# Backward pass of a windowed attention: set-up, first four quads and last weight gradients in another form

## The chip, the core and the metric

The kernel runs on one core of a Trainium2 chip. A core has five engines with their own instruction streams: TensorE (PE) multiplies and transposes into PSUM, VectorE (DVE) and ScalarE (ACT) copy results out of PSUM and compute element by element, GpSimd (POOL) and SyncE (SP) here mostly issue DMAs; ACT issues some too. All DMAs of a core share 16 DMA engines. The metric is the device time of one execution in microseconds, lower is better: the median of several runs.

## The reference

The input x is an image of 256 x 256 pixels with C = 384 channels in bf16. It is cut into 1024 windows of 8 x 8 pixels; each window attends to itself, with one head. The kernel returns the output and the three gradients for a given `grad_out`.

```python
qkv = xw @ wqkv                       # xw: 1024 windows x 64 x 384
q, k, v = qkv[..., :C], qkv[..., C:2*C], qkv[..., 2*C:]
p = softmax(einsum('bqc,bkc->bqk', q, k) * C ** -0.5)
o = einsum('bqk,bkc->bqc', p, v) @ wo
out, vjp = jax.vjp(forward, x, wqkv, wo)
return out, *vjp(grad_out)            # d x, d wqkv, d wo
```

## The kernel before

**Algebra.** The weights are folded once: A = Wq Wk^T times the scale, AT is its transpose, B = Wv Wo, BT its transpose (C x C each, `A_sb`, `AT_sb`, `B_sb`, `BT_sb`). Scores are then x A x^T, the output P x B, and every gradient needs only x, `grad_out` and these four. The folding needs transposes of the three parts of `w_sb` (`wT`) and, for the end, of `wo_sb` (`woT_sb`): 36 transposes of 128 x 128 on TensorE against the identity `ident`, each group of three copied out of a PSUM bank by VectorE, and then four products of nine matmuls (L93 to L102).

**Quads.** The work goes over 128 quads. A quad is four tiles of 128 pixels, two windows each. `load` fetches x into `xq` (four DMAs of 96 KB on SP's queue) and `grad_out` into `dq` (four on POOL's). `load_turn` turns both into `dT` and `xT` (channels on the partitions) by two DMA transposes on SP's queue; the test on `G_ON_PE`, which is 0, leaves all of it to DMA, and `grad_turn`, which would do it on TensorE, does nothing.

**Steps.** `step(c, b, a, ahead)` handles three quads at once in an order written out by hand, which holds on every engine (`manual_schedule`): the quad b gets its scores (`sd`, 24 small matmuls), the softmax and its gradient on VectorE and ScalarE (`soft`, six parts), and `uq` and `vq` (x B and x AT, 24 matmuls of 384 columns, copied out by ScalarE); the quad a, one ahead, gets `z` (`project` kind 0: BT on `dT`, nine matmuls of 512 columns) and `y` (kind 1: A on `xT`, 18 of half the rows); both land in `yz`, which SP's queue turns into `tok`; the quad c, one behind, gets `attend`, which makes the output and d x and stores them from POOL's queue, and leaves `Uq` and `Wq`. `turn` sends the probabilities and their gradient (`ps`) through another DMA transpose on SP's queue to `PS`. The order of b's part, with the places that matter here:

```python
B(scores); B(soft, 0)
B(uv, 0, 0); B(uv, 0, 1); B(soft, 1)
B(uv, 1, 0); B(uv, 1, 1); B(soft, 2); B(soft, 3)
B(uv, 2, 0); B(uv, 2, 1)
for t in range(QUAD): A(grad_turn, t)
B(uv, 3, 0); B(uv, 3, 1); B(soft, 4)
for mo in range(CK): A(project, 0, mo)
B(soft, 5); B(turn)
```

So step i has on SP's queue, in this order: `dT` and `xT` of quad i + 2, `PS` of quad i, the loads of quad i + 3, `tok` of quad i + 1. A DMA that has to wait holds up all behind it on its queue.

**Weight gradients.** `gf_group` sums x^T U and x^T W over three quads into `GF_acc` (f32), in six pieces of 12 matmuls; `filler` puts two pieces into each step from step 4 on. The last group has only two quads. After the loop `filler` runs what is left, and then the code from L380 on casts `GF_acc` to `GFb`, turns it into `GFT` on TensorE, multiplies with the weights (27 and 9 matmuls) and stores d wqkv in three row blocks and d wo in one.

All PSUM tiles come from `ring`, eight banks.

Of the kernel before, what the change touches and what calls it, by code (L numbers as in the profile page):

```python
# [8 lines left out]
ACT = mybir.ActivationFunctionType  # L9
ALU = mybir.AluOpType  # L10
AX = mybir.AxisListType
BF16 = mybir.dt.bfloat16
F32 = mybir.dt.float32
# [9 lines left out]
def kernel(  # L23
# [33 lines left out]
    ring = ctx.enter_context(tc.tile_pool(name="ring", bufs=8, space=bass.MemoryType.PSUM))  # L57

    ident = const.tile([P, P], BF16)
    make_identity(nc, ident[:])  # L60

    w_sb = const.tile([P, CK, J], BF16)
    nc.sync.dma_start(out=w_sb[:], in_=wqkv.rearrange("(m p) j -> p m j", p=P))
    wo_sb = grp.tile([P, CK, C], BF16, tag="Wq", name="wo_sb")
    nc.scalar.dma_start(out=wo_sb[:], in_=wo.rearrange("(m p) n -> p m n", p=P))

    wT = []
    for part in range(3):
        dst = grp.tile([P, CK, C], BF16, tag="Uq", name="wT")
        for k in range(CK):  # L70
            jm = part * CK + k
            pt = ring.tile([P, C], BF16, tag="r")
            for m in range(CK):
                nc.tensor.transpose(pt[:, m * P:(m + 1) * P], w_sb[:, m, jm * P:(jm + 1) * P], ident[:])
            nc.vector.tensor_copy(out=dst[:, k, :], in_=pt[:])
        wT.append(dst)
    woT_sb = const.tile([P, CK, C], BF16)
    for mo in range(CK):
        pt = ring.tile([P, C], BF16, tag="r")
        for m in range(CK):  # L80
            nc.tensor.transpose(pt[:, m * P:(m + 1) * P], wo_sb[:, m, mo * P:(mo + 1) * P], ident[:])
        nc.vector.tensor_copy(out=woT_sb[:, mo, :], in_=pt[:])

    A_sb = const.tile([P, CK, C], BF16)
    AT_sb = const.tile([P, CK, C], BF16)
    B_sb = const.tile([P, CK, C], BF16)
    BT_sb = const.tile([P, CK, C], BF16)
    for dst, left, right, sc in (
        (BT_sb, wo_sb, wT[2], None),
        (A_sb, wT[0], wT[1], scale),  # L90
        (B_sb, wT[2], wo_sb, None),
        (AT_sb, wT[1], wT[0], scale),
    ):  # L93
        for mr in range(CK):
            pc = ring.tile([P, C], F32, tag="r")
            for mc in range(CK):
                nc.tensor.matmul(pc[:], lhsT=left[:, mc, mr * P:(mr + 1) * P], rhs=right[:, mc, :],
                                 start=(mc == 0), stop=(mc == CK - 1))
            if sc is None:
                nc.vector.tensor_copy(out=dst[:, mr, :], in_=pc[:])  # L100
            else:
                nc.scalar.activation(out=dst[:, mr, :], in_=pc[:], func=ACT.Copy, scale=sc)  # L102

    GF_acc = const.tile([P, 2, CK, C], F32)
    nc.vector.memset(GF_acc[:], 0.0)

    def windows(ap, st, first, count=2):
        row, col = st["at"]
# [10 lines left out]
            nc.gpsimd.dma_start(out=dq[:, t, :], in_=windows(grad_out, st, 2 * t))  # L119

    def load_turn(st):
        xq, dq = st["xq"], st["dq"]
        st["xT"] = xT = qp.tile([P, QUAD, CK, P], BF16, tag="xT", name="xT", bufs=3)
        st["dT"] = dT = qp.tile([P, QUAD, CK, P], BF16, tag="dT", name="dT")
        for src, dst in ((dq, dT), (xq, xT)):
            k = G_ON_PE if src is dq else 0
            if k < QUAD:
                nc.sync.dma_start_transpose(out=dst[:, k:].rearrange("p t m k -> p (t m) k"),
                                            in_=src[:, k:].rearrange("p t c -> p (t c)"))

    def grad_turn(st, t):
        if t >= G_ON_PE:
            return
        pt = ring.tile([P, CK, P], BF16, tag="r")
        for m in range(CK):
            nc.tensor.transpose(pt[:, m, :], st["dq"][:, t, m * P:(m + 1) * P], ident[:])
        nc.vector.tensor_copy(out=st["dT"][:, t, :, :], in_=pt[:])

    ALL = False
    split = [ALL]  # L140
# [152 lines left out]

    fill = []

    def gf_group(sts):
        n = len(sts) * QUAD
        for f in range(2):
            for ma in range(CK):
                pw = ring.tile([P, C], F32, tag="r", name="pg")  # L300
                for i in range(n):
                    st, t = sts[i // QUAD], i % QUAD
                    product(pw[:], st["xq"][:, t, ma * P:(ma + 1) * P], st["UW"[f] + "q"][:, t, :], i == 0, i == n - 1)
                nc.vector.tensor_tensor(out=GF_acc[:, f, ma, :], in0=pw[:], in1=GF_acc[:, f, ma, :], op=ALU.add)  # L304
                yield

    def filler(n):
# [7 lines left out]
    def step(c, b, a, ahead):  # L315


        def on(st):
            return (lambda f, *r: f(st, *r)) if st is not None else (lambda f, *r: None)
        C_, B, A = on(c), on(b), on(a)  # L320
        B(scores)
        B(soft, 0)
        B(uv, 0, 0)
        B(uv, 0, 1)
        B(soft, 1)
        B(uv, 1, 0)
        B(uv, 1, 1)
        B(soft, 2)
        B(soft, 3)
        B(uv, 2, 0)  # L330
        B(uv, 2, 1)
        for t in range(QUAD):
            A(grad_turn, t)
        B(uv, 3, 0)
        B(uv, 3, 1)
        B(soft, 4)
        for mo in range(CK):
            A(project, 0, mo)
        B(soft, 5)
        B(turn)  # L340
        if ahead is not None:
            load(ahead)
        filler(1)
        C_(attend, (0, 1))
        split[0] = True
        for mo in range(CK):
            A(project, 1, mo)
        A(to_tokens)
        filler(1)
        split[0] = ALL  # L350
        C_(attend, (2, 3))

    G_ON_PE = 0
    EV = {"z": "AAA", "y": "AAA", "u": "AAAA", "v": "AAAA", "o": "AAAA", "U": "DDDD", "W": "DDDD", "d": "AAAA"}
    quads = [(row, col) for row in range(0, H, 2 * WIN * QUAD) for col in range(0, W, WIN)]
    sts = [{"at": q, "i": i} for i, q in enumerate(quads)]
    n = len(sts)
    AHEAD = 3
    with tc.manual_schedule(engines=MANUAL):
        for i in range(min(AHEAD, n)):  # L360
            load(sts[i])
            if i < AHEAD - 1:
                load_turn(sts[i])
        held = []
        get = lambda i: sts[i] if 0 <= i < n else None
        for i in range(-1, n + 1):
            if AHEAD - 1 <= i + AHEAD - 1 < n:
                load_turn(sts[i + AHEAD - 1])
            step(get(i - 1), get(i), get(i + 1), get(i + AHEAD) if i >= 0 else None)
            if i > 0:  # L370
                held.append(sts[i - 1])
                sts[i - 1] = None
            if held and (len(held) == GQ or i == n):
                fill.append(gf_group(held))
                held = []
        split[0] = False
        filler(1 << 30)

    GFb, GFT = [], []
    for f in range(2):  # L380
        GFb.append(grp.tile([P, CK, C], BF16, tag="Uq", name="GFb"))
        GFT.append(grp.tile([P, CK, C], BF16, tag="Wq", name="GFT"))
        nc.vector.tensor_copy(out=GFb[f][:], in_=GF_acc[:, f, :, :])
        for mb in range(CK):
            pt = ring.tile([P, C], BF16, tag="r")
            for ma in range(CK):
                nc.tensor.transpose(pt[:, ma * P:(ma + 1) * P], GFb[f][:, ma, mb * P:(mb + 1) * P], ident[:])
            nc.vector.tensor_copy(out=GFT[f][:, mb, :], in_=pt[:])
    dw_view = out_2.rearrange("(m p) j -> p m j", p=P)
    for ma in range(CK):  # L390
        dw_sb = grp.tile([P, J], BF16, tag="xq", name="dw_sb", bufs=2 * GQ + 4)
        for i, (lhs, rhs, r0) in enumerate(((GFT[0], w_sb, C), (GFb[0], w_sb, 0), (GFT[1], woT_sb, 0))):
            pe = ring.tile([P, C], F32, tag="r")
            for mb in range(CK):
                nc.tensor.matmul(pe[:], lhsT=lhs[:, mb, ma * P:(ma + 1) * P], rhs=rhs[:, mb, r0:r0 + C],
                                 start=(mb == 0), stop=(mb == CK - 1))
            if i < 2:
                nc.scalar.activation(out=dw_sb[:, i * C:(i + 1) * C], in_=pe[:], func=ACT.Copy, scale=scale)
            else:
                nc.vector.tensor_copy(out=dw_sb[:, i * C:(i + 1) * C], in_=pe[:])  # L400
        nc.sync.dma_start(out=dw_view[:, ma, :], in_=dw_sb[:])
    dwo_sb = qp.tile([P, QUAD, C], BF16, tag="dq", name="dwo_sb", bufs=6)
    for mc in range(CK):
        pe = ring.tile([P, C], F32, tag="r")
        for ma in range(CK):
            nc.tensor.matmul(pe[:], lhsT=w_sb[:, ma, 2 * C + mc * P:2 * C + (mc + 1) * P], rhs=GFb[1][:, ma, :],
                             start=(ma == 0), stop=(ma == CK - 1))
        nc.vector.tensor_copy(out=dwo_sb[:, mc, :], in_=pe[:])
    nc.sync.dma_start(out=out_3.rearrange("(m p) n -> p m n", p=P), in_=dwo_sb[:, 0:CK, :])


# [28 lines left out]
```

## Time and profile before

| What | us |
|---|---|
| median of 7 runs | 1996.82 (1994.23 to 2000.95) |
| time of the profiled execution | 1995.6 |
| its span, first to last instruction | 1993.5 |
| TensorE busy | 1961.8 |
| ScalarE busy | 1453.8 |
| VectorE busy | 1258.2 |
| first transpose of weights on TensorE | at 6.32 |
| first `y` projection | at 19.84 |
| sum of the last gradient group on VectorE begun | at 1980.95 |
| last store issued | at 1990.17 |

The page of the profile gives busy time of each engine, the span in 40 slices, the DMA queues, and the chain of work that ended last. TensorE's time is the sum of matmuls whose ends are modelled, so being busy does not mean being at its peak. A row of a timeline reads: start, duration, engine, line, operation, output <- input, count, and in brackets the idle time before it with what ended it; on SP's queue the duration is the time for which the issue held the queue. The windows give busy time by stretch, with the granted TensorE clock as a share of full speed.

### The profile page before, as it was taken

What the parts mean: (1) busy time and instruction counts of PE and PEld (TensorE: products, weight loads), DVE (VectorE), ACT (ScalarE), POOL (GpSimd) and SP (SyncE); (2) the same over time, 40 slices, a digit from 0 to 9 for tenths busy, and PEclk for the clock granted to TensorE, in tenths of its full rate; (3) what the DMA queues carried; (4) which work ended last, traced back from release to release, by engine and by line L of the source; (5) the groups of instructions that cost most, each with busy time, mean ns of one, the idle gap of its engine ahead of it and who ended that gap; (6) DMA issues with size and microseconds to landing.
All of it is one profiled execution on the core that took longest, in us unless ns stands there. A gap on an engine that the chain in (4) does not pass through costs nothing.

```text
span 1993.5 us, 52374 instructions
## 1 busy us (share of the span) xinstructions
PE 1961.8 (98%) x19418; PEld 1123.2 (56%) x19418; DVE 1258.2 (63%) x2851; ACT 1453.8 (73%) x3341; POOL 1122.6 (56%) x2054
## 2 busy tenths in 40 slices
PE   7999999999999999999999999999999999999998
PEld 4455555555555555555555555555555555555555
DVE  4666666566666666666666666666666666666665
ACT  5777777677777777777777777777777777777774
POOL 3655555555555555555655565555555555555643
PEclk9999999999999999999999999999999999999999
DMA  9999999999999999999999999999999999999993
GB/s 198 216 216 226 210 223 209 210 217 221 211 223 216 222 209 215 220 224 211 227 211 214 223 206 224 220 219 219 220 216 214 209 224 219 220 218 215 216 207 100
DMA packets 1042272, 425.62 MB, mean 214 GB/s; under 512 B 925792, under 2 KB 1016672, under 8 KB 1042016
## 3 DMA queue, kind: packets, MB, share of 16 engines
q1 hardware_dynamic: 943312, 270.60, 81.4%
q0 software_dynamic: 98304, 151.39, 31.1%
q8 instruction: 152, 2.49, 0.5%
q14 instruction: 104, 0.85, 0.1%
q10 hardware_dynamic: 400, 0.29, 0.0%
HBM read 101.84 MB, written 101.84 MB: 102 GB/s over the span
## 4 chain that ended last, share of the span: by engine, by line
PE 90%; DMA 7%; ACT 1%; DVE 1%; issue 0%; SPq 0%; POOL 0%; ACTq 0%; POOLq 0%
PE pj L147 33%; PE pj L145 12%; PE pg L147 12%; PE pg L145 11%; PE pd L258 6%; PE pu L253 5%; PE sd L147 5%; PE pw L253 4%; DMA dT<-dq 4%; DMA PS<-ps 1%; DMA dq<-in_grad_out_dram 1%; ACT uq L229 0%; DMA xT<-xq 0%; ACT vq L229 0%; PE pd L253 0%
## 5 line engine op out<-in xcount | busy, mean ns | idle before, releaser
L292 POOL DMA_DIRECT2D out_dram<-o x256 | 139.1, 543 | 691.9 <-ACT o L264 679.7
L304 DVE TENSOR_TENSOR GF_acc<-pg,GF_acc 128x384 f32<-128x384 f32 x258 | 143.9, 558 | 527.2 <-PE pg L145 372.2
L264 ACT CAST o<-po 128x384 bf16<-128x384 f32 x512 | 221.4, 487 | 248.1 <-issue 247.7
L147 PEld LDWEIGHTS <-xT 128*128 128x128 bf16 x3072 | 291.7, 98 | 182.3
L147 PE MATMUL pj<-AT_sb,xT 128*128 128x384 bf16 x1536 | 333.5, 326 | 0.0
L147 PE MATMUL pj<-B_sb,xT 128*128 128x384 bf16 x1536 | 333.5, 326 | 0.0
L119 POOL DMA_DIRECT2D dq<-in_grad_out_dram x512 | 274.2, 547 | 72.4 <-DMA out_dram<-o 39.9
L147 PE MATMUL pj<-dT,BT_sb 128*128 128x512 bf16 x1152 | 269.7, 379 | 11.2 <-DMA dT<-dq 10.1
L145 PE MATMUL pj<-xT,A_sb 128*64 128x512 bf16 x2304 | 272.0, 381 | 1.9 <-DMA xT<-xq 1.9
L229 ACT CAST uq<-pj 128x384 bf16<-128x384 f32 x512 | 247.3, 483 | 31.7 <-PE pj L147 28.5
L229 ACT CAST vq<-pj 128x384 bf16<-128x384 f32 x512 | 250.1, 488 | 2.7 <-ACT uq L229 0.3
L264 ACT CAST d<-pd 128x384 bf16<-128x384 f32 x512 | 227.6, 512 | 0.2 <-ACT o L264 0.2
L147 PEld LDWEIGHTS <-xq 128*128 128x128 bf16 x1572 | 153.5, 98 | 115.0 <-issue 0.3
L145 PEld LDWEIGHTS <-xq 128*64 128x64 bf16 x3000 | 167.8, 110 | 88.9
L207 ACT COPY ps<-Pb 64x256 bf16<-64x256 bf16 x256 | 103.2, 403 | 149.7 <-DVE Pb L204 148.2
L163 ACT CAST yz<-pj 128x512 bf16<-128x512 f32 x384 | 208.5, 659 | 3.7 <-PE pj L145 3.6
L161 ACT CAST yz<-pj 128x512 bf16<-128x512 f32 x384 | 206.7, 644 | 2.3 <-issue 1.8
L145 PEld LDWEIGHTS <-A_sb 128*64 128x64 bf16 x2304 | 132.5, 110 | 100.1 <-DMA xT<-xq 2.3
L147 PEld LDWEIGHTS <-BT_sb 128*128 128x128 bf16 x1152 | 111.3, 98 | 137.1 <-DMA dT<-dq 17.0
L147 PE MATMUL pg<-Uq,xq 128*128 128x384 bf16 x1032 | 181.6, 326 | 0.0
L253 PE MATMUL pu<-xq,PS 64*64 64x384 bf16 x1024 | 175.3, 335 | 3.9 <-DMA PS<-ps 3.4
L258 PE MATMUL pd<-tok,ps 128*64 128x384 bf16 x1024 | 177.8, 344 | 0.0
(68 smaller groups left out, 3368.5 us busy)
## 6 DMA issues: line engine op xcount, KB each, us to landing
xq<-in_x_dram SPq DMA_DIRECT2D x512, 96.0 KB, 4.1
dq<-in_grad_out_dram POOLq DMA_DIRECT2D x512, 96.0 KB, 3.9
out_dram<-o POOLq DMA_DIRECT2D x256, 96.0 KB, 4.3
out_dram<-o POOLq DMA_DIRECT2D x512, 48.0 KB, 4.4
out_dram<-d POOLq DMA_DIRECT2D x256, 96.0 KB, 4.5
out_dram<-d POOLq DMA_DIRECT2D x512, 48.0 KB, 4.4
dT<-dq SPq DMA_TRANSPOSE x128, 6.4
xT<-xq SPq DMA_TRANSPOSE x128, 6.7
```

The lines of the kernel that those rows point to most:

```text
L119: nc.gpsimd.dma_start(out=dq[:, t, :], in_=windows(grad_out, st, 2 * t))
L145: nc.tensor.matmul(out[h], lhsT=lhsT[:, h], rhs=rhs, start=start, stop=stop)
L147: nc.tensor.matmul(out, lhsT=lhsT, rhs=rhs, start=start, stop=stop)
L161: ENG[EV["z"][mo]](out=yz[:, mo, :, 0:4:3, :], in_=pj[:])
L163: ENG[EV["y"][mo]](out=yz[:, mo, :, 1:3, :], in_=pj[:])
L207: nc.scalar.copy(out=ps[h, :, w, :], in_=Pb[h, :, :])
L229: cp(out=dst[:, t, :], in_=pj[:])
L253: nc.tensor.matmul(at[o, :], lhsT=turned(st, lhs, t, h), rhs=st[rhs][h, t, :], **{"start": True, "stop": True, **fl})
L258: nc.tensor.matmul(pd[outer if w == 0 else 1 - outer][o, :], lhsT=st["ps"][:, t, w, :], rhs=st["tok"][:, :, t, w, :], **flags)
L264: nc.scalar.copy(out=sb[:], in_=src[outer][:])
L292: nc.gpsimd.dma_start(out=windows(dst, st, 2 * t0 + 1), in_=sb[:])
L304: nc.vector.tensor_tensor(out=GF_acc[:, f, ma, :], in0=pw[:], in1=GF_acc[:, f, ma, :], op=ALU.add)
```

## The change

- **Weights.** `w_sb` comes in three column parts: the last one first on SP's queue, the other two on ACT's queue behind `wo_sb`. The three loads of x for quads 0 to 2 follow at once on SP's queue; `ident` is made after the first four loads of `dq` are issued.
- **Warm-up.** Nine matmuls on zeros, whose results nobody reads, before the first transpose.
- **Order of the set-up.** `wT[2]`, BT, the turn of quad 0's `dq` and x on TensorE, `wT[0]`, `wT[1]`, A, then the memset of `GF_acc`. B and AT (`weight_rest`) come in step 0 behind scores and `soft` 0; the transposes for `woT_sb` come in step 0 behind `z`.
- **Turning.** `G_ON_PE` = 4 and `X_ON_PE` = 1 now count quads: the gradient of quads 0 to 3 and x of quad 0 are turned by TensorE (12 transposes and four copies each) instead of by DMA; those of quads 1 to 3 at the place of `grad_turn` in steps 0 to 2. From quad 4 on nothing is changed.
- **Copies.** Those of the set-up and of the turns alternate between VectorE and ScalarE (`copy_out`).
- **End.** The last group casts each row of `GF_acc` at once (`final`); transposes and weight products are put between its pieces and behind it, by parts; d wqkv goes out in two column parts and three rows of the third, on two queues, d wo before those rows.

```diff
+    def fetch_weights():
+        nc.sync.dma_start(out=w_sb[:, :, columns(2)], in_=w_in[:, :, columns(2)])
+        nc.scalar.dma_start(out=wo_sb[:], in_=wo.rearrange("(m p) n -> p m n", p=P))
+        for k in (0, 1):
+            nc.scalar.dma_start(out=w_sb[:, :, columns(k)], in_=w_in[:, :, columns(k)])
+
+    def warm_up(n):
+        zero = B_sb[:].rearrange("p m c -> p (m c)")[:, 0:4 * P]
+        nc.vector.memset(zero, 0.0)
+        for i in range(n):
+            pt = ring.tile([P, 4 * P], F32, tag="r", name="warm")
+            nc.tensor.matmul(pt[:], lhsT=zero[:, 0:P], rhs=zero, start=True, stop=True)
+
+    def copy_out(i, out, in_):
+        if i % 2:
+            nc.scalar.copy(out=out, in_=in_)
+        else:
+            nc.vector.tensor_copy(out=out, in_=in_)
...
+    def weight_rest():
+        weight_product(B_sb, wT[2], wo_sb, None)
+        weight_product(AT_sb, wT[1], wT[0], scale)
...
-        for src, dst in ((dq, dT), (xq, xT)):
-            k = G_ON_PE if src is dq else 0
-            if k < QUAD:
-                nc.sync.dma_start_transpose(out=dst[:, k:].rearrange("p t m k -> p (t m) k"),
-                                            in_=src[:, k:].rearrange("p t c -> p (t c)"))
+        for src, dst, on_pe in (("dq", "dT", G_ON_PE), ("xq", "xT", X_ON_PE)):
+            if st["i"] >= on_pe:
+                nc.sync.dma_start_transpose(out=st[dst][:].rearrange("p t m k -> p (t m) k"),
+                                            in_=st[src][:].rearrange("p t c -> p (t c)"))
+
+    def turn_on_pe(st, src, dst):
+        for t in range(QUAD):
+            pt = ring.tile([P, CK, P], BF16, tag="r", name="pt")
+            for m in range(CK):
+                nc.tensor.transpose(pt[:, m, :], st[src][:, t, m * P:(m + 1) * P], ident[:])
+            copy_out(t, st[dst][:, t, :, :], pt[:])
+
+    def grad_turn(st):
+        if 0 < st["i"] < G_ON_PE:
+            turn_on_pe(st, "dq", "dT")
...
         B(soft, 0)
+        if b is not None and c is None:
+            weight_rest()
...
-        for t in range(QUAD):
-            A(grad_turn, t)
+        A(grad_turn)
...
             A(project, 0, mo)
+        if b is not None and c is None:
+            turn_blocks(woT_sb, wo_sb)
...
-    G_ON_PE = 0
+    G_ON_PE, X_ON_PE = 4, 1
...
+    def weight_gradients(group):
...
+        for i in range(CK + 1):
+            next(group)
+        turn_blocks(GFT[0], final[0])
+        for i in range(CK - 1):
+            next(group)
+        for part, left, right in ((0, GFT[0], w_sb[:, :, columns(1)]), (1, final[0], w_sb[:, :, columns(0)])):
+            dw = rows("dw")
+            for k in range(CK):
+                product_row(k, dw[:, k, :], left, right, scale)
+            nc.sync.dma_start(out=dw_out[:, :, columns(part)], in_=dw[:])
+        turn_blocks(GFT[1], final[1])
+        dwo = rows("dwo")
+        for k in range(CK):
+            product_row(k, dwo[:, k, :], w_sb[:, :, columns(2)], final[1], None)
+        nc.sync.dma_start(out=dwo_out, in_=dwo[:])
+        dw = rows("dw")
+        for k in range(CK):
+            product_row(k, dw[:, k, :], GFT[1], woT_sb, None)
+            (nc.scalar, nc.sync)[k % 2].dma_start(out=dw_out[:, k, columns(2)], in_=dw[:, k, :])
+
     with tc.manual_schedule(engines=MANUAL):
-        for i in range(min(AHEAD, n)):
-            load(sts[i])
-            if i < AHEAD - 1:
-                load_turn(sts[i])
+        fetch_weights()
+        warm_up(9)
+        load(sts[0])
+        make_identity(nc, ident[:])
+        load(sts[1])
+        load(sts[2])
+        load_turn(sts[0])
+        load_turn(sts[1])
+        turn_blocks(wT[2], w_sb, 2 * CK)
+        weight_product(BT_sb, wo_sb, wT[2], None)
+        turn_on_pe(sts[0], "dq", "dT")
+        turn_on_pe(sts[0], "xq", "xT")
+        turn_blocks(wT[0], w_sb, 0)
+        turn_blocks(wT[1], w_sb, CK)
+        weight_product(A_sb, wT[0], wT[1], scale)
+        nc.vector.memset(GF_acc[:], 0.0)
...
-            if held and (len(held) == GQ or i == n):
+            if held and i == n:
+                last = gf_group(held, True)
+            elif len(held) == GQ:
                 fill.append(gf_group(held))
                 held = []
```

## The prediction

> **What bounds the kernel now.** I read the page first: the busy times, the slices, the chain of waits. TensorE is busy 98% of the span, so only two places can give much: where it isn't busy, and where it runs slowly.
>
> ```profile
> span 1993.5 us, 52374 instructions
> PE 1961.8 (98%) x19418; PEld 1123.2 (56%) x19418; DVE 1258.2 (63%) x2851; ACT 1453.8 (73%) x3341; POOL 1122.6 (56%) x2054
> ...
> PE   7999999999999999999999999999999999999998
> ```
>
> Only the first and the last slice are below 9. Next, the waits of TensorE alone, longest first (us in total, times, longest): all its waits together are some 26 us, and the weights, `dT`, `PS` and `xT` head them.
>
> ```profile
> PE pj L147 <- DMA dT<-dq: 10.1, 8, 3.6
> PE pt L74 <- DMA w_sb<-in_wqkv_dram: 6.3, 1, 6.3
> PE pu L253 <- DMA PS<-ps: 3.4, 3, 2.5
> PE pj L145 <- DMA xT<-xq: 1.9, 1, 1.9
> ...
> PE pt L387 <- DVE GFb L383: 1.6, 1, 1.6
> ```
>
> Then the timeline of VectorE, of which I took the first row maximum of each quad (`mx`, L187) as a clock of the steps: 23.51, 33.85, 46.94, 59.98, 77.60, 92.87, 108.45. Quads 2 and 3 stand 13.1 and 13.0 apart (no gradient filler yet), the next gap is 17.62, and from quad 5 on most gaps are 15.13; ten of the remaining gaps are longer by more than 0.3 us, and all the excess is 12.9 us. So steady steps are bound by TensorE, and the loss sits in the first 78 us and behind the last step. The windows of busy time, cut at these maxima (start:end, length, then busy us of each engine, granted clock, DMA share, GB/s), show where:
>
> ```profile
> 0.00:6.30 6.30, 0.00 (x0) 0.00 (x0) 1.98 (x1) 1.28 (x1) 5.02 (x14) 1.00 0.72 227
> 6.30:23.50 17.20, 14.89 (x125) 9.94 (x126) 6.89 (x18) 6.44 (x12) 6.24 (x12) 1.00 1.11 223
> ...
> 60.00:77.60 17.60, 13.48 (x118) 7.03 (x117) 8.66 (x21) 11.76 (x26) 8.91 (x17) 0.90 1.16 218
> 77.60:92.90 15.30, 15.30 (x153) 8.66 (x152) 9.73 (x23) 11.29 (x26) 8.78 (x17) 1.00 1.19 220
> ```
>
> Last, the timeline of TensorE inside the long gap:
>
> ```profile
> 65.25 2.12 PE L147 MATMUL pj<-dT,BT_sb 128*128 128x512 bf16 x9 [1.61 <-DMA dT<-dq]
> ...
> 70.11 0.35 PE L253 MATMUL pu<-xq,PS 64*64 64x384 bf16 x1 [2.46 <-DMA PS<-ps]
> ...
> 71.29 3.82 PE L145 MATMUL pj<-xT,A_sb 128*64 128x512 bf16 x18
> ```
>
> TensorE waits for quad 4's `dT`, then for quad 2's `PS`; and after the two pauses 18 projections take 3.82 us that take 2.11 in every other step: the granted clock fell (0.90 above). SP's queue is late there: it issues that `dT` at 58.73 and that `PS` at 64.72, behind `tok` (5.39 us of the queue), `dT` and `xT`.
>
> **The change, part by part**, against the profiled execution (span 1993.5, its time 1995.6, which is 1.2 under the median 1996.82).
>
> (a) *Up to the first maximum.* Now 23.51: first the whole `w_sb` (6.32), 36 transposes in 3.7 us, 36 products in 5.8, and `y` starts only when `xT` has come, at 19.84; the maximum follows 3.67 later. In the change: nine warm-up products of 512 columns. The 18 rows at 3.82 above, two to a full width, give 0.42 each at the low clock: 3.8 us from about 1.6 (memset first), to 5.5. The last third of the weights, 288 KB, is not in the trace as a load of its own: the nearest row is `wo_sb`, 288 KB, 5.9 us to landing beside the 864 KB; 96 KB loads take 4 to 6. Between 4.0 and 6.6; I take 6.0. From there, TensorE in order: 9 transposes 0.7 (nine take 0.68 at L387) and a copy 0.5, BT 1.5, 12 turns of `dq` 0.9, which gives 9.6; `xq`'s fourth load is issued at about 3.5 and takes 6.1, so 9.7 as well; 12 turns of x 0.9, 18 transposes 1.3 and a copy 0.5, A 1.5, z 1.95: y starts at 15.8, and the maximum comes at 15.8 + 3.67 = 19.5. **-4.0** (from -1.5, if loads are late by 2.5, to -6).
> The chip's notes speak against this part. The Trainium skill, TensorE: Matmul & The Clock Gate, Part 4, says that transposes don't count as activity for the clock gate; the change strings up to 42 of them together. By that rule A, z and y (27 full-width products, 5.3 us) could run at half clock, up to 3.4 us (its window) dearer, and (a) would be -0.6. But the row: 36 transposes from 6.32, the first 27 in 3.06 us (0.11 each, against 0.07 in the tail, so at the low clock), and the nine products that follow at 10.03 take 1.63, as everywhere later, with no product before them. Transposes did lift the clock here. I go by the row.
>
> (b) *Step 0* takes in what was ahead: B and AT, 18 products of 0.163 = 2.9 us, stand between scores and `uq`. ScalarE's `ex` stands behind the copies of `uq`/`vq` of two tiles, so all the softmax chain moves by 2.9 + 0.2. Its four copies for B and AT lie under the products. Then ScalarE runs from 27.53 to 32.94 without a pause and sets the next scores; into this stretch come two copies of `dT` and one of `woT`, 3 x 0.48 = 1.4. TensorE's 21 transposes lie beside that. **+4.6** (from +1.4, if the products hide in ScalarE's stretch, to +5.6).
>
> (c) *Steps 1 and 2* gain 12 turns each (0.7 to 0.9 us of TensorE) and two copies each on ScalarE (0.37 in a burst to 0.48) and on VectorE (0.3). ScalarE is busy 11.1 to 11.2 of 13.0 us there and its z copies hold TensorE up: 0.9 each. **+1.8** (1.4 to 2.4).
>
> (d) *The long gap.* Four `dT` transposes and one `xT` leave SP's queue; each holds it 1.4 to 3.0 us, and the quads 0 and 1 also wait for loads in it (6.4 us at `dq`). SP then meets `tok` of quad 2 when its `yz` is there (last copy from 43.48, 1.72 us for three) instead of at 53.12, some 8 us later; quad 4's `dT` goes out about 9 us ahead of 58.73 relative to its use, and quad 2's `PS` 3 us or more. Both waits go, and with them the low clock: 17.62 becomes 13.04. What is late next is ScalarE, already in the 13.04. **-4.6** (0 to -4.6). The same lead covers the excess of quads 5 and 6 (0.14, 0.45): **-0.6** (0 to -1.8, with quad 8's 1.17). Behind that, queue and order per step are as before, and I expect the same 15.13.
>
> (e) *The tail.* Now from the last gradient product (1980.59) to the end, 1993.5, is 12.9: VectorE's chain with 1.61 idle on TensorE, 27 + 9 products, three serial copies (1.53), a store (3.3 from issue to end). In the change nine transposes move ahead of the last two groups; behind: 0.5 for those, 18 products 2.9, nine transposes 0.5, 18 products 2.9, one copy 0.8 with its latency, 3.2 for a smaller store (96 KB land in about 2.0, 288 in 2.3): 10.8. The new casts `final` (about 0.3 each) lie under 1.3 us groups. **-2.1** (-1.3 to -2.6; the split copies have ScalarE free, 13.9 idle there).
>
> Sum: -4.0 + 4.6 + 1.8 - 4.6 - 0.6 - 2.1 = **-4.9**: 1990.7 for an execution like the profiled one, and 1996.8 - 4.9 = **1991.9** at the median.
>
> **Rivals.**
> R1, *more is hidden*. If the 18 products of (b) lie beside ScalarE's stretch, it costs 1.4: -8.1, 1988.7. For: TensorE is busy only 9.18 of 10.4 us in that window. Against: `ex` is in order behind `uq`, which is behind the products.
> R2, *the wait changes its name*. The DMA share is 1.10 and more in every window; if `PS` or `tok` lands late although issued early, (d) gives nothing: -4.9 + 5.2 = +0.3, 1997.1; half of it gives 1994.5. For: 2.46 us of the gap were `PS`, not `dT`. Against: its lateness was issue, 64.72.
> R3, *slower*: `dT` in the loop. SP issues it only 4 to 6 us ahead of the step that uses it, landing takes 6.4, the use is 4.6 into the step. Where a late one strikes, it costs 0.6 to 3.7 us, 1.2 on average over ten steps. Another phase of SP against POOL's stores could leave less slack; from eight more such steps on the change is slower by 4 us; ten give 1991.9 + 12 = 2004. Against: the order within a step is unchanged, and after stalls the slack grows again within ten steps.
>
> **How the numbers follow.** A measurement of this kernel can tell about 0.2% (4 us) from no change. My forecast -4.9 has 0.55; with (a) and (b) uncertain by 2 us, 0.40 of it is beyond 4 us and 0.15 within. R1 0.20, faster. R2 0.17, within. R3 0.08, slower. So faster 0.60, same 0.32, slower 0.08. The range takes R1 with a quieter loop (-12) and R2's full loss: 1985 to 1998; the forecast's own is 1988.5 to 1995.
>
> **What would show it.** Right: the first maximum near 19.5; gaps of about 15, 14, 14 and 13 behind it, quad 4's maximum near 75.4 instead of 77.60; granted clock 1.0 there; 18 `A_sb` rows in 2.1; about 11 us behind the last gradient product. Wrong: a first maximum over 22 (loads or clock), a wait for `PS`, `tok` or `dT` in the first 80 us, or an excess of the loop far from 12.9 us.

## The result, and the profile after

The changed kernel takes 1992.11 us at the median (27 runs, 1985.71 to 2000.0), the kernel before, run beside it, 1995.4 (63 runs, 1988.15 to 2009.81); the ratio is 0.9979, with a 95% interval of 0.9968 to 0.9991. So it is faster by about 0.2%, 1.8 to 6.4 us; the forecast, -4.9, lies inside.

The two profiles are further apart than that. The page of the changed kernel begins:

```profile
span 1984.9 us, 52529 instructions
PE 1965.8 (99%) x19487; PEld 1126.1 (57%) x19487; DVE 1259.9 (63%) x2860; ACT 1461.6 (74%) x3357; POOL 1122.7 (57%) x2054
...
PE   8999999999999999999999999999999999999999
```

The span is 8.6 us shorter, and the last slice of TensorE is 9 now. But this execution took 1986.72, 5.4 under its kernel's median, while the one of before was at its own. Cutting both spans at the same marks, the first row maximum of each quad, shows which part of the 8.6 belongs to the change:

| Stretch | forecast | before | after | difference |
|---|---|---|---|---|
| start to first maximum | -4.0 | 23.51 | 19.40 | -4.1 |
| step 0 | +4.6 | 10.34 | 15.67 | +5.3 |
| steps 1 and 2 | +1.8 | 26.13 | 28.70 | +2.6 |
| step 3, the long gap | -4.6 | 17.62 | 12.95 | -4.7 |
| steps 4 to 7 | -0.6 | 61.11 | 60.68 | -0.4 |
| quad 8 to quad 127, where nothing was changed | 0 | 1812.9 | 1807.6 | -5.3 |
| last first maximum to the end | -2.1 | 41.9 | 40.0 | -1.9 |

Without the untouched stretch the sum is -3.25, and the medians differ by 3.3. That they agree so closely is luck, for each stretch is taken from one execution of each kernel, and the first alone varies by 1.8 us among profiles with the new set-up. What happens in the untouched stretch is shown below: it varies by over 15 us among profiles of the same loop.

TensorE's waits in the first 80 us of the changed kernel, longest first:

```profile
PE pj L156 <- ACT dT L89: 4.8, 3, 1.6
PE warm L85 <- DVE B_sb L82: 1.2, 1, 1.2
PE sd L156 <- ACT yz L172: 0.9, 2, 0.4
PE pt L141 <- DMA dq<-in_grad_out_dram: 0.8, 1, 0.8
```

The waits for `w_sb`, `xT`, `PS` and quad 4's `dT` are gone from it. A new one heads it, three times 1.6 us: `z` now waits for ScalarE's copies of the turned gradient. The timeline of step 0 shows one of them:

```profile
27.93 0.88 ACT L89 COPY dT<-pt 128x384 bf16<-128x384 bf16 x2
...
28.87 2.10 PE L156 MATMUL pj<-dT,BT_sb 128*128 128x512 bf16 x9 [1.58 <-ACT dT L89]
```

The transposes were finished at 25.9; their copies stand on ScalarE behind `ex`, `ps`, `uq` and `vq`. And the windows, cut at the maxima:

```profile
19.40:35.10 15.70, 13.41 (x116) 7.94 (x115) 7.32 (x20) 11.36 (x24) 0.00 (x0) 1.00 0.51 97
35.10:49.50 14.40, 12.46 (x130) 6.97 (x129) 9.09 (x23) 12.16 (x28) 4.01 (x8) 1.00 0.81 172
49.50:63.80 14.30, 12.35 (x129) 6.91 (x128) 9.13 (x23) 12.34 (x28) 8.75 (x17) 1.00 1.15 220
63.80:76.70 12.90, 12.40 (x117) 6.39 (x116) 8.72 (x20) 11.18 (x26) 8.60 (x16) 1.00 1.20 204
```

In all four the granted clock is 1.00. The first three carry the turns; TensorE is idle 1.9 to 2.3 us in each, and only 0.5 in the fourth.

### The profile page after: what moved, and what is told of

It is laid out like the page before. It is cut to its first block, busy times and chain, and to the rows that moved or that the text cites. A ratio compares the mean times of both kernels' runs of the same rounds, so it can differ in the third digit from the quotient of the medians.

```text
span 1984.9 us, 52529 instructions
## 1 busy us (share of the span) xinstructions
PE 1965.8 (99%) x19487; PEld 1126.1 (57%) x19487; DVE 1259.9 (63%) x2860; ACT 1461.6 (74%) x3357; POOL 1122.7 (57%) x2054
## 4 chain that ended last, share of the span: by engine, by line
PE 93%; DMA 4%; issue 2%; POOL 1%; ACT 0%; DVE 0%; ACTq 0%; POOLq 0%
PE pj L156 35%; PE pg L156 13%; PE pj L154 12%; PE pg L154 12%; PE pd L267 6%; PE pu L262 5%; PE sd L156 5%; PE pw L262 4%; DMA dT<-dq 2%; DMA PS<-ps 1%; POOL dq L127 0%; DMA out_dram<-o 0%; PE pd L262 0%; DMA dq<-in_grad_out_dram 0%; DMA out_dram<-d 0%
```

## The experiments

Times of single stretches are taken from the profile of each run; the ratios are those of several runs against the kernel before, with their 95% intervals. The kernels without warm-up and with B's products back in the set-up ran once each and have no ratio; there only stretches of the profile are read. The excess of the loop is the time from quad 4's first maximum to quad 127's, less 123 steps of 15.13.

### The new end alone

The kernel before with `gf_group(held, True)` and `weight_gradients(last)` in place of its end:

```diff
-    GFb, GFT = [], []
-    for f in range(2):
...
+        weight_gradients(last)
```

> The kernel before with the new end alone (last group with its casts at once, products between its pieces, stores by parts). Theory 'set-up and end each keep their own gain': the first maxima stay where they are before (23.5, 33.9, 46.9, 60.0, 77.6, each within 0.5 us), and from the last quad's first maximum to the end of the span it is 39.9 us instead of 41.9, so about -2.0 us or 0.9990. Rival 'the gain is the set-up's, the end only shifts': 41 us or more from the last maximum to the end, ratio 1.000.

From the last maximum to the end it is 39.7 us (41.9 before), quad 4's maximum is at 77.53 (77.60). The marks between did not all stay within 0.5 us: they are 22.92, 33.26, 46.35 and 61.36. Steps 2 and 3 lose about as much as before, but in other places: they take 15.02 and 16.17 instead of 13.04 and 17.62, with waits of 3.31 and 2.20 us for `PS` and only 0.63 for `dT`. So which transpose is late, and where, differs between executions. The ratio is 0.9972 (0.9951 to 0.9993), whose interval holds the -2.2. The end gives about what it gives in the whole change, and nothing in the set-up depends on it.

### The copies of the turned gradients on VectorE

```diff
-            copy_out(t, st[dst][:, t, :, :], pt[:])
+            (copy_out if st["i"] == 0 else on_vector)(t, st[dst][:, t, :, :], pt[:])
```

> The changed kernel, with the copies of quads 1 to 3's turned gradients all on VectorE instead of alternating. Theory 'ScalarE's copies of dT hold up z': the 4.8 us that TensorE waits for dT of ScalarE go down to under 2, steps 0, 1 and 2 take 14.7, 13.5 and 13.4 us instead of 15.67, 14.42 and 14.28, quad 4's maximum comes at about 74 instead of 76.7. Rival 'the turns themselves are the cost, or VectorE is as late': the three steps stay within 0.4 us of the changed kernel's.

Steps 0 to 3 take 14.24, 13.08, 12.88 and 12.89; quad 4's maximum is at 74.15, although the first one came at 21.06 this time. TensorE no longer waits for `dT` of ScalarE at all; what is left is 0.8 for VectorE. Ratio 0.9962 (0.9948 to 0.9977), an interval that overlaps the changed kernel's: the gain is read from the steps. Steps 1 and 2 are as long as before the change, where no turn was in them: 12 transposes on TensorE cost nothing there. All of (c) was the place of the copies.

### Only quad 0's gradient on TensorE

```diff
-    G_ON_PE, X_ON_PE = 4, 1
+    G_ON_PE, X_ON_PE = 1, 1
```

> The changed kernel with the gradient of quad 0 alone on TensorE; those of quads 1 to 3 are turned by DMA again. Theory 'the long gap came from SP's queue starting late': quad 4's dT is still issued 3 us or more before its step begins (changed kernel 10.0, before 1.2), step 3 stays at 13.0, steps 0, 1 and 2 take 14.3, 13.1 and 13.0, and quad 4's maximum comes at about 72.8. Rival 'the gap came from the DMA transposes themselves': step 3 takes 15 us or more again with waits for dT or PS in it, and quad 4's maximum is at 75 or later.

Neither theory had it whole. Step 3 is 12.89 and quad 4's maximum comes at 73.22, as the first said. But step 4 takes 19.09 instead of 15.28. The gap was not removed, it came a step later. The timeline of TensorE, and the windows of that step:

```profile
78.84 3.64 PE L156 MATMUL pj<-dT,BT_sb 128*128 128x512 bf16 x9 [1.95 <-DMA dT<-dq]
```

```profile
78.00:81.00 3.00, 2.16 (x7) 0.83 (x8) 1.63 (x4) 2.11 (x5) 1.65 (x4) 0.71 0.97 271
81.00:84.00 3.00, 3.00 (x14) 1.49 (x13) 0.00 (x0) 1.17 (x2) 0.00 (x0) 0.72 1.19 236
```

It is the same picture as before the change: a wait for `dT`, here quad 5's, and then nine products in 3.64 us that take 2.1 elsewhere, at a granted clock of 0.71. The times at which SP's queue issues `dT` say why. Counted from the first maximum of the quad before, the issues for quads 2, 3, 4 and 5 come 8.9, 6.8, 5.1 and 2.4 us ahead. The queue loses 1.6 to 2.8 us in each of these steps, which have no filler: `dT` of quads 3 to 5 goes out at 40.62, 55.18 and 70.78, with no pause in the queue between, so a round of transposes and loads takes 14.6 and 15.6 us, and the step lasts 13. Steps 0 to 2 are 13.65, 13.08 and 12.88: beside the run above, where the turns stayed on TensorE, step 0 is 0.6 shorter, the others the same. So the transposes of quad 1, with VectorE's copies, still cost something in step 0.

### The gradients of quads 0 to 3 on TensorE, and nothing else

The kernel before, set-up and end untouched; `grad_turn` keeps VectorE's copies:

```diff
-            k = G_ON_PE if src is dq else 0
-            if k < QUAD:
+            k = 0
+            if src is xq or st["i"] >= G_ON_PE:
...
-        if t >= G_ON_PE:
+        if st["i"] >= G_ON_PE:
...
-    G_ON_PE = 0
+    G_ON_PE = 4
```

> The kernel before, with one part of the change alone: the gradient of quads 0 to 3 is turned on TensorE, at the place of grad_turn, with VectorE's copies; set-up, order and end stay. Theory 'in steps without filler (13.0 us) SP's queue needs more than a step (14 to 15 us), so its lead runs out; each dT less gives it 2 us back': step 3 is 13.0 instead of 17.62, steps 1 and 2 stay within 0.3 us of 13.1, and quad 4's maximum comes at 71 to 73.5 instead of 77.6: more than the whole change gains there (76.7). Rival 'the loads of the first quads in the old order are what makes the queue late': step 3 or 4 is over 15.5.

The steps take 10.8, 13.09, 13.04 and 12.88, and quad 4's maximum comes at 74.08 against 77.60: one part alone gains 3.5 us there, where the whole change gains 0.9. SP's queue, which issued quad 4's `dT` at 58.73, does so earlier here:

```profile
46.57 6.66 SPq L167 DMA_TRANSPOSE tok<-yz  x1
53.46 1.69 SPq L128 DMA_TRANSPOSE dT<-dq  x1
55.37 2.87 SPq L128 DMA_TRANSPOSE xT<-xq  x1
58.41 1.19 SPq L233 DMA_TRANSPOSE PS<-ps  x1
```

That is 7.7 us ahead of its step instead of 1.2, and `PS` goes out at 58.41 instead of 64.72, without the new order of the loads. Quad 4's maximum was expected at 73.5 at the latest; it is later because the first one is, at 24.27 (23.51 before): quad 0's turn stands behind all the weight products in TensorE's order, and `z` waits 0.74 for its copies. Ratio 0.9974 (0.9960 to 0.9988), as good as the whole change.

### No warm-up

```diff
         fetch_weights()
-        warm_up(9)
         load(sts[0])
```

> The changed kernel without the nine warm-up products. Theory 'transposes count for the clock, and the loads of dq and x set the first 10.6 us anyway': BT's nine products are slow (about 3 us), quad 0's turns wait for the same loads, and the first maximum moves from 19.4 by less than 1 us. Rival 'transposes do not count': the clock is still low at A, z and y, and the first maximum is 2.5 to 3.5 us later.

The first maximum moves from 19.40 to 19.63. The timeline of TensorE:

```profile
5.06 1.14 PE L97 MATMUL pt<-ident,w_sb 128*128 128x128 bf16 x9 [5.06 <-DMA w_sb<-in_wqkv_dram]
6.01 3.16 PE L104 MATMUL pc<-wT,wo_sb 128*128 128x384 bf16 x9
8.96 1.49 PE L141 MATMUL pt<-ident,dq 128*128 128x128 bf16 x12
10.24 0.98 PE L141 MATMUL pt<-ident,xq 128*128 128x128 bf16 x12
11.06 1.17 PE L97 MATMUL pt<-ident,w_sb 128*128 128x128 bf16 x18
12.44 1.65 PE L104 MATMUL pc<-wT 128*128 128x384 bf16 x9 [0.21 <-DVE wT L91]
```

BT's nine products run at the low clock (3.16), and it costs nearly nothing, for in the changed kernel TensorE waits for `dq` and x until 10.65. From 11.06 on all is at full speed. BT's products lie ahead of the transposes here, so this run doesn't say which of the two lifted the clock; the kernel before, with its transposes and no product ahead of its first full-speed product, does.

### B's products back in the set-up

```diff
         weight_product(BT_sb, wo_sb, wT[2], None)
+        weight_product(B_sb, wT[2], wo_sb, None)
...
     def weight_rest():
-        weight_product(B_sb, wT[2], wo_sb, None)
         weight_product(AT_sb, wT[1], wT[0], scale)
```

> The changed kernel with the nine products of B back in the set-up, right behind BT, where TensorE waits for loads of dq and x anyway (7.7 to 10.65). Theory 'work put behind the first scores is only moved, and costs more there than in the wait for loads': the first maximum comes at 19.4 to 21, step 0 falls from 15.67 to 14.2, quad 4's maximum is about 1 us earlier for the same first maximum. Rival 'it is conserved': the first maximum is 1.5 us later and step 0 1.5 us shorter.

The first maximum stays (19.58), so the nine products fit into the wait for loads, as expected. But step 0 does not shorten: 15.89. The softmax did move 1.2 us ahead (`ex` at 23.50 instead of 24.77), and then:

```profile
25.00:27.50 2.50, 0.73 (x4) 0.29 (x3) 1.74 (x6) 2.39 (x7) 0.00 (x0) 1.00 0.37 67
27.50:29.50 2.00, 1.91 (x7) 0.74 (x7) 0.00 (x0) 1.39 (x4) 0.00 (x0) 0.70 0.00 0
29.50:32.00 2.50, 2.50 (x15) 1.44 (x15) 0.45 (x2) 1.56 (x3) 0.00 (x0) 0.56 0.00 0
```

While ScalarE's copies hold up `z`, TensorE is busy 0.73 of 2.5 us, and the clock falls to 0.70 and 0.56: `z` takes 3.34 us instead of 2.1. The same copies cost 1.6 us of waiting in the changed kernel without that; here they cost what the early B had brought.

### The three edits together

VectorE's copies, B in the set-up, and the last three rows on the other queue each, so that ScalarE's last copy doesn't stand behind the issue of a store:

```diff
-            (nc.scalar, nc.sync)[k % 2].dma_start(out=dw_out[:, k, columns(2)], in_=dw[:, k, :])
+            (nc.sync, nc.scalar)[k % 2].dma_start(out=dw_out[:, k, columns(2)], in_=dw[:, k, :])
```

> The changed kernel with VectorE's copies for the turns of quads 1 to 3, B's products back in the set-up behind BT, and the end's three row stores on the other of the two queues each (SP, ACT, SP), so that ScalarE's copy does not stand behind an issue. Theory 'the parts add': first maximum 19.4 to 21, steps 12.8, 13.1, 12.9, 12.9, quad 4's maximum 71 to 73, end 39.6; about -8 us against before, ratio 0.996. Rival 'SP's lead is used up sooner by the shorter steps': one of steps 3 to 5 is over 16 with a wait for dT, and the ratio is 0.998.

First maximum 19.31, steps 12.77, 13.08, 12.89, 12.89, quad 4's maximum 70.94 (76.72 in the changed kernel, 77.60 before), end 39.8. Ratio 0.9937 (0.9915 to 0.9960): faster than the kernel before, and its interval lies below that of the changed kernel. The stretches account for 6.7 us and 2.1, so for 0.9956, inside the interval. The windows of steps 0 to 2:

```profile
19.30:32.10 12.80, 11.94 (x107) 7.06 (x106) 6.83 (x20) 9.83 (x21) 0.00 (x0) 1.00 0.62 119
32.10:45.20 13.10, 12.66 (x130) 7.06 (x129) 9.66 (x25) 11.24 (x26) 4.09 (x8) 1.00 0.85 182
45.20:58.00 12.80, 12.36 (x129) 6.84 (x127) 9.59 (x24) 11.19 (x26) 8.54 (x16) 1.00 1.14 220
```

TensorE is idle 0.9 us in step 0 instead of 2.3, and 0.4 in steps 1 and 2 instead of 1.9. With the copies moved, the early B brings 1.47 (14.24 to 12.77), its nine products exactly. The other order of the stores brings at most 0.2.

### The loads of x on POOL's queue

```diff
-            nc.sync.dma_start(out=xq[:, t, :], in_=windows(x, st, 2 * t))
+            (nc.sync if st["i"] < 4 else nc.gpsimd).dma_start(out=xq[:, t, :], in_=windows(x, st, 2 * t))
```

> The same, and from quad 4 on the loads of x are issued from POOL's queue instead of SP's. It asks what makes the ten or so long steps of the loop. Theory 'SP's queue is the limit: it never pauses and issues dT only some 5 us ahead': with 2.8 us less in it per step its lead grows to 10 us or more, the loop's excess over 15.13 a step falls from 7 to 17 us to under 4, ratio about 0.991. Rival 'the 16 engines behind all queues are the limit': the lead stays at 4 to 6 us and the excess at 7 us or more, ratio as for e7_three_edits.

Neither: ratio 1.1267 (1.1227 to 1.1307). SP's queue, which paused for 0.6 us at most in the loop of the changed kernel, now waits, by its own list of waits (100 to 1900 us):

```profile
SPq L133 <- DMA dq<-in_grad_out_dram: 379.6, 114, 7.3
```

Loads of `dq` come late to nearly every step; they are behind x and the stores on POOL's queue. `tok` holds SP's queue for 6.49 us at the median, 4.8 in the changed kernel. So the question stays open; what the run says is that these loads are not to be put on POOL's queue here.

### Each dT a step earlier

The three edits, and three `dT` tiles, loads four steps ahead:

```diff
-    AHEAD = 3
+    AHEAD = 4
...
             if 0 <= i < n - 3:
+                grad_load_turn(sts[i + 3])
```

> The kernel with the three edits, and in the loop each dT is turned one step earlier (three dT tiles, loads four steps ahead, 11 xq tiles). It asks whether the loop's excess is the short slack of dT or the queue as a whole. Theory 'dT has the least slack': waits for dT vanish from the loop, PS and tok keep theirs, and the excess over 15.13 a step falls from 7 to 18 us (nine profiles with the same loop) to 3 us or less; 5 us or more faster than e7_three_edits. Rival 'the queue as a whole is late, the next in it waits instead': PS or tok or xT take the waits, the excess stays at 7 us or more, and the time is that of e7_three_edits within 3 us.

> e7_three_edits once more, as the measure beside e9_dT_a_step_earlier on the same chip and as a second sample of the same program's loop: the first maxima and the end within 0.5 us of the first profile from 19.3, 70.9 and 39.7 (the first maximum may move by up to 2 us with the loads), the loop's excess anywhere from 7 to 18 us, ratio 0.994 to 0.996.

The second theory was right. `dT` is issued 19 to 23 us ahead and is waited for no more, but `PS` is, TensorE's waits from 80 us on:

```profile
PE pu L268 <- DMA PS<-ps: 7.7, 8, 1.9
```

The excess is 10.2 us, the ratio 0.9957 (0.9942 to 0.9972). The three edits run again give 0.9942 (0.9920 to 0.9964), with marks at 20.05, 71.68 and 39.8 - and an excess of 2.7 us, where the same program had 9.4 before. The excess of all profiles with this loop and SP's queue as it is (the POOL run left out): before 13.0, new end 11.7, turns alone 13.2; changed kernel 7.3, no warm-up 16.9, B in the set-up 18.4, VectorE's copies 8.2; three edits 9.4 and 2.7; only quad 0 turned 13.2, with step 4's 3.8 in it. It follows no edit. TensorE's waits in the loop, most of them for `dT` and `PS`, sum to 2.2 us in the quietest of these profiles and 15.1 in the noisiest. In three of them the clock fell to half for 3.41 us besides: once without warm-up, once with `dT` a step earlier, twice with one turned quad. What sets the size in one execution was not found.

## Why the prediction was right

**The bound.** "The loss sits in the first 78 us and behind the last step": both gains are there, and the loop's step stayed at 15.13.

**(a)** -4.0 forecast, -4.1 measured. The terms differ: the weights came at 5.1, not 6.0, and `dq` was waited for until 9.6, x until 10.65. In this profile the loads, not the warm-up, set the mark: without the warm-up it is at 19.63. The forecast counted the warm-up as the start of a chain that the loads cut anyway.

On transposes the row that the prediction went by was right, and not the rule that it set against it (the Trainium skill, TensorE: Matmul & The Clock Gate, Part 4): in the kernel before, the trace has the full clock from 9.91, behind 3.6 us of transposes and 0.12 us ahead of the first product. (The 1.00 that the windows give ahead of that says nothing: no record of the clock stands there yet, and the first 27 transposes run at 0.11 us each.)

But the forecast reckoned with a clock that stays up once it is lifted, and that held in the profile shown by luck. Of the eight profiles with the new set-up and the warm-up, two have the first maximum at 21.06 and 20.71 instead of 19.3 to 20.05. One is that with VectorE's copies:

```profile
7.74:11.16 3.42, 1.70 (x22) 1.16 (x22) 1.77 (x5) 1.34 (x3) 2.02 (x4) 1.00 1.07 301
11.16:14.57 3.41, 3.41 (x26) 2.59 (x25) 1.79 (x5) 1.58 (x4) 3.03 (x7) 0.50 1.09 316
```

The full clock came early there, at 4.33. In the first window TensorE waited 1.2 us for `dq` and was busy 1.70, and behind it the clock stood at half for 3.41 us. The 18 transposes for A take 2.13 us instead of 1.17, A's nine products 2.36 instead of 1.65. In the other, that with one turned quad, they take 1.98 and 2.54. From the first of these transposes to `z` it is 4.1 to 4.2 us in both instead of 2.9: 1.3 us lost. The prediction put such a loss at up to 3.4, but half the clock for 3.4 us can cost no more than 1.7.

**(b)** +4.6 forecast, +5.3 measured. The term that was mis-sized is the copies: "two copies of `dT` and one of `woT`, 3 x 0.48 = 1.4". The two of `dT` alone cost 1.43 (15.67 to 14.24 when they go to VectorE), because `z` waits for them, and ScalarE's work for `z` with it; and the 12 transposes, which the forecast laid beside ScalarE's stretch at no cost, cost 0.6 with their copies on VectorE (14.24 against 13.65). The products cost 1.47 for B's nine, as counted.

**(c)** +1.8 forecast, +2.6 measured: the same error. The prediction was right that ScalarE is the limit there, but its "0.9 each" priced the copies by their duration, not by what is queued behind them: 1.3 each. The turns themselves cost nothing in these two steps, as steps of 13.08 and 12.88 show.

**(d)** -4.6 forecast, -4.7 measured, and the mechanism holds: `dT` and `PS` were late by issue. What the prediction put beside it, the waits for loads in SP's queue and its late start, is not needed: with the old set-up the gap goes as well, and with the new set-up and three more DMA transposes it comes back one step later. What counts is how much the queue has to do in a step of 13 us.

**(e)** -2.1 forecast, -1.9 measured (-2.2 with the new end alone). TensorE's wait of 1.6 us for `GFb` is gone from its list, and 10.5 us follow the last gradient product, where the forecast had 10.8 (12.9 before).

**The rivals.** R1 did not come: the products are on the path. R2 did not come in the changed kernel; one of its kind did in the run with one turned quad. R3's mechanism is there all the time: late `dT` and `PS` in the loop, with an excess of 2.7 to 18.4 us an execution, as chance has it. It is what makes the profile's -8.6 and the medians' -3.3 differ, and was taken into the range.

So the forecast of 1991.9 for a median of 1992.11 is close, and partly by luck in the level: before stood at 1996.82 in the runs shown and at 1995.4 in the runs beside the change. The difference, -4.9, was too large by 1.6 against the medians, and by as much against the profile's stretches, where (b) and (c) make 1.5 of it.

## What to carry to other kernels

When work is moved from a DMA to TensorE, ask first which engine copies the result out of PSUM and what stands behind that copy: here the transposes with VectorE's copies cost 0.6 us in one step and nothing in two, and the copies on the busier engine cost 4 us until they went to the other one. A queue that keeps up in a long step can fall behind in the short steps of the start, and the wait appears some steps later, at another tile; so take its load per step against the length of that step. And compare stretches between marks that both programs have, before a difference of two spans is given to a change: here 5.3 of 8.6 us lay in a loop that was not touched.

## What the hardware showed that was not expected

SP's queue drifts to the same lead from both sides. It issues `dT` 10.0 us ahead of its step at quad 4 of the changed kernel and 1.2 us ahead before the change; ten to twelve steps later both are at 3 to 6, and stay between about 3 and 7 in all of the loop, without a pause of more than 0.6 us in the queue. The shortest rows of a step's issues add up to 10.4 us there (`tok` 3.9, `dT` 1.4, `xT` 1.4, `PS` 1.2, loads 2.5), the mean rows to some 14.4. What holds the lead there was not tried.

The same pause of 1.6 us before `z` cost another 1.2 us of low clock in the run with B in the set-up, and nothing in the changed kernel. The traces' records of the clock show how that can be: in each execution all its changes lie a whole multiple of 3.41 us apart, and where this grid lies differs from one execution to the next. Cut on their own grids, the windows with the pause in them are these, first of the run with B in the set-up, then of the changed kernel:

```profile
24.89:28.30 3.41, 1.55 (x9) 0.64 (x7) 1.85 (x6) 3.19 (x8) 0.00 (x0) 1.00 0.31 56
26.69:30.10 3.41, 1.83 (x9) 0.81 (x9) 1.32 (x4) 3.24 (x9) 0.00 (x0) 1.00 0.00 0
```

Behind the first the clock is at 0.50 for 3.41 us, behind the second it stays at 1.00: the grid cut the pause at another place. How busy a window has to be is not settled by this: one of 1.50 us (354.66 in the kernel before) was not followed by a low clock, and that of the set-up with 1.70 us of transposes was.
